# The last 64 keys of two successive pairs of heads in four 64x64 quadrants of TensorE

## The chip, the cores and the metric

The kernel runs on one core of one Trainium2 chip. The metric is the device time of one run in microseconds, the median of three runs.

## The reference

Attention with a sigmoid in place of the softmax, for 8 batches of 12 heads, 448 positions and 64 values a head:

```python
scores = scale * np.matmul(q, k.transpose(0, 1, 3, 2)) - np.log(S)   # scale 1/8, S 448
attn = 1.0 / (1.0 + np.exp(-scores))
x = np.matmul(attn, v)                                               # (8, 12, 448, 64)
```

The heads are put side by side (x is 8 x 448 x 768 then). Behind it stands a mixing of positions through rank 32 and a feed forward of width 3072:

```python
h = x.transpose(0, 2, 1) @ U @ V            # U 448 x 32, V 32 x 448
u = x + h.transpose(0, 2, 1)
out = u + np.maximum(u @ w_ch1, 0.0) @ w_ch2   # 768 x 3072, 3072 x 768
```

The keys of a head are 448 = 3 x 128 + 64: three full blocks and the last 64.

## The kernel before, in words

**Layout.** Everything is held transposed: features on the 128 partitions, the 448 positions as columns. Two heads of 64 features fill the partitions, so a batch has six pairs of heads, and one tile of 128 x 448 for each. The sigmoids of one block of 128 keys stand with the keys on the partitions and two heads' 448 positions side by side as columns (128 x 896).

**Attention of one pair** (`pair`, with `scores_of` and `values_of`). The scores of a block of keys (L500) take, for each head, the 64 partitions of that head; the two heads' matmuls use the upper and the lower half of the array's rows. ACT makes the sigmoid of each head (L588). The values of the first three blocks (L514) use all 128 rows, and each head 64 of the columns, both into one bank. The last 64 keys are the fourth block, j = 3: its score matmul yields 64 rows for each head, its two sigmoids have 64 partitions each, head 0 in the upper and head 1 in the lower half of one 128 x 448 tile, and its value matmul (L519) is one full 128 x 128 matmul for both heads, with a v tile that the host has laid out with zeros in the other head's places. ACT copies the result bank into the pair's tile of u (`ua` or `ub`), and for batches 1 to 7 DVE takes its maximum.

Batches 0 and 1 do this in float32. Batches 2 to 7 split every operand into two float16 halves, high and low, after scaling, and do three products (high by high, low by high, high by low) in place of one. For this POOL writes the high half (`scaled`) and DVE the rest (`rest`, L367) of q, k and v into a staging buffer `stg` (two buffers, all of a pair's halves in one), after ACT has summed absolute values to find the scales (`bound`, L420, whose wide output is written to a tile `junk` that nothing reads). The sigmoids are split too: L609 copies the high half on ACT, L367 writes the rest on DVE.

**Mixing** (L660 to L762). Once a batch's pairs are in u, they are transposed (xnt holds the transposed halves), multiplied with U and V, and added to u; u is then split into halves `us` for the feed forward.

**Feed forward.** W1 and W2 come as int64 words that hold float64 values. In batch 0, `decode` loads each group's weights in pieces of 128 x 768 words (`w`<-`w_in`, L344, through a ring of three buffers `w64`), DVE packs them to float32 (`to_f32`, two operations a piece), ACT bounds them (L420), and DVE and ACT split them to halves; they are also stored to scratch memory and read back for the later batches. Batches 0 to 3 run the plain products: 18 matmuls a chain in L836 (W1), 12 a chain in L856 (W2), six groups of weights a batch, W1 of a group one step ahead of its W2. Batches 4 to 7 are done two at a time by a scheme of seven products on quarters (L1031) at the end of the program, where no attention is left.

**What sets the order.** The program is written as a list of operations, each with an engine, a cost in us that is a number of the table at the top or at the call, a position in time (`pos`), and the tiles it reads and writes. `Plan.order` places them: it repeatedly takes the engine that can start first, and on it, of the operations that could start by then, the one with the least position. A tile gets its buffer out of a ring when its first user is placed. The result is a fixed order of instructions for each engine, and a fixed order of DMA issues on SP; at run time each engine works its list off in this order and waits where something is late. TensorE's operations carry the shape of array they begin and end with (`modes`): a change of shape costs `SWITCH` in the plan, and while the array is in a smaller shape an operation that begins with the same one is preferred by `BOND`.

The attention of batch 0 is at the start of the program, that of batch 1 beside the feed forward of batch 0, and those of 2, 4, 3, 5, 6, 7 beside the feed forward of batches 1 to 3. Eight banks of results are shared: the feed forward has four while batch 0 runs and three later (`PF`), attention the other four, and later five (`PS_`). The sigmoid tiles have six buffers for the wide blocks and two for the narrow one (`A2`, `A1`), the float32 ones before the split two and one (`AT2`, `AT1`).

## Time and profile before

| | |
|---|---|
| runs | 1572.27, 1572.36, 1574.84 us |
| median | 1572.36 us |
| the profiled execution's own time | 1575.69 us |
| its span in the profile | 1573.9 us |
| TensorE busy | 1550.3 us (99%), 8711 matmuls |
| VectorE (DVE) | 1129.4 us (72%) |
| ScalarE (ACT) | 850.6 us (54%) |
| GpSimd (POOL) | 381.4 us (24%) |
| DMA | 319.37 MB, 203 GB/s on average |
| TensorE's granted clock | 0.997 |

The profile is one execution. The span runs from its first to its last instruction; the time of the run is 1.8 us more. Tile names in the rows are the program's. Their buffer number is left out where a group holds several. A row with a line number in its form "x18" stands for a run of 18 like instructions.

### The profile page before, as it was taken

Reading aid. Unit: us, or ns where it says so; the run is one execution under the profiler, and the core shown is the slowest. Engines: PE = TensorE matmul, PEld = TensorE weight load, DVE = VectorE, ACT = ScalarE, POOL = GpSimd, SP = SyncE. Lnnn points to the kernel's source line nnn. Section 1 sums busy time; section 2 is a strip of 40 time slices with the busy share of each in tenths; the row PEclk is TensorE's granted clock in tenths of the full one; section 3 lists DMA queues with packets and bytes.
Section 4 is the critical chain, followed back from the end, with each engine's and each line's share of the span. In section 5 each row is a group of like instructions: output and inputs, shape, how many; then the busy total and the mean of one; then the engine's idle time right before and its main releaser. Section 6 shows DMA issues by size and latency. Waiting matters only on the chain.

```text
span 1573.9 us, 23648 instructions
## 1 busy us (share of the span) xinstructions
PE 1550.3 (99%) x8711; PEld 764.0 (49%) x8711; DVE 1129.4 (72%) x1886; ACT 850.6 (54%) x1521; POOL 381.4 (24%) x465
## 2 busy tenths in 40 slices
PE   8999999999999999999999999999999899999999
PEld 3344455544444544444444445555555455555554
DVE  2899999766777768777677766687776668564656
ACT  7666755478687668687698763242332614121310
POOL 0100001741222552132122254246551500000000
PEclk9999999999999999999999999999999999999999
DMA  8698888988867788655677549977673573333321
GB/s 231 191 315 280 282 291 254 317 233 196 206 192 184 222 261 225 159 154 160 187 211 189 144 149 285 315 246 247 220 248 126 176 255 132 106 109 136 107 106 71
DMA packets 208724, 319.37 MB, mean 203 GB/s; under 512 B 126176, under 2 KB 174688, under 8 KB 196320
## 3 DMA queue, kind: packets, MB, share of 16 engines
q1 hardware_dynamic: 208608, 317.86, 65.2%
q8 instruction: 68, 1.11, 0.3%
q14 instruction: 48, 0.39, 0.1%
HBM read 246.25 MB, written 77.42 MB: 206 GB/s over the span
## 4 chain that ended last, share of the span: by engine, by line
PE 91%; DVE 3%; DMA 2%; issue 1%; POOL 1%; SPq 1%; ACT 1%; POOLq 0%; DVEq 0%; ACTq 0%
PE bank L1031 36%; PE bank L856 20%; PE bank L836 19%; PE bank L500 7%; PE bank L514 5%; PE bank L519 2%; DMA w<-w_in 2%; PE bank L753 1%; DMA v__102<-v_in 1%; SPq L344 1%; DVE stg__107 L367 1%; PE bank L762 0%; DVE us__87 L367 0%; DVE xnt L367 0%; DVE us__86 L367 0%
## 5 line engine op out<-in xcount | busy, mean ns | idle before, releaser
L367 DVE SCALAR_TENSOR_TENSOR a<-at,a 128x896 f16<-128x896 f32 (+1 forms) x144 | 142.0, 1004 | 38.6 <-ACT a L609 38.2
L856 PE MATMUL bank<-h__93,w__91 128*128 128x448 f16 x792 | 159.9, 355 | 0.0
L856 PE MATMUL bank<-h__92,w__90 128*128 128x448 f16 x792 | 158.8, 353 | 0.0
L836 PEld LDWEIGHTS <-w__89 128*128 128x128 f16 x936 | 90.5, 98 | 89.4 <-issue 7.6
L856 PEld LDWEIGHTS <-w__91 128*128 128x128 f16 x864 | 83.6, 98 | 82.8 <-issue 9.1
L856 PEld LDWEIGHTS <-w__90 128*128 128x128 f16 x864 | 83.1, 98 | 82.1 <-issue 7.7
L609 ACT ACTIVATE a<-at 128x896 f16<-128x896 f32 (+1 forms) x144 | 116.9, 858 | 0.4
L1031 PEld LDWEIGHTS <-w__88 128*128 128x128 f16 x819 | 80.1, 98 | 74.7
L836 PEld LDWEIGHTS <-w__88 128*128 128x128 f16 x792 | 76.8, 98 | 74.6 <-issue 4.6
L1031 PEld LDWEIGHTS <-w__91 128*128 128x128 f16 x756 | 74.0, 98 | 74.0 <-issue 5.2
L1031 PEld LDWEIGHTS <-w__89 128*128 128x128 f16 x756 | 74.0, 98 | 69.0
L919 POOL TENSOR_TENSOR w<-w 128x384 f32<-128x384 f32 x96 | 104.7, 1091 | 5.1
L836 PE MATMUL bank<-us__87,w__89 128*128 128x448 f16 x504 | 99.7, 353 | 0.0
L1031 PEld LDWEIGHTS <-w__90 128*128 128x128 f16 x693 | 67.8, 98 | 63.3
L836 PE MATMUL bank<-us__86,w__89 128*128 128x448 f16 x432 | 85.3, 353 | 1.7 <-DVE ua__75 L367 1.7
L836 PE MATMUL bank<-us__86,w__88 128*128 128x448 f16 x432 | 84.8, 353 | 0.0
L588 ACT ACTIVATE at<-bank,bias_s,c__221 128x448 f32<-128x448 f32 (+1 forms) x96 | 65.0, 723 | 16.4 <-PE bank L500 7.0
L915 POOL TENSOR_TENSOR w<-w 128x384 f32<-128x384 f16 x48 | 45.7, 981 | 112.9 <-DVE xnt L923 70.6
L836 PE MATMUL bank<-us__87,w__88 128*128 128x448 f16 x360 | 70.9, 353 | 0.0
L588 ACT ACTIVATE at<-bank,bias_s,c__223 128x448 f32<-128x448 f32 (+1 forms) x96 | 64.5, 724 | 10.7 <-PE bank L500 10.0
L588 ACT ACTIVATE at<-bank,bias_s,c__222 128x448 f32<-128x448 f32 (+1 forms) x96 | 65.1, 722 | 5.9 <-DVE a L367 2.6
L843 ACT ACTIVATE r__94<-bank 128x448 f32<-128x448 f32 x48 | 25.9, 539 | 64.9 <-PE bank L836 64.9
(1167 smaller groups left out, 3130.2 us busy)
## 6 DMA issues: line engine op xcount, KB each, us to landing
w<-w_in SPq DMA_DIRECT2D x48, 768.0 KB, 5.9
forms<-xnt SPq DMA_DIRECT2D x24, 768.0 KB, 4.8
w__88<-forms SPq DMA_DIRECT2D x13, 1344.0 KB, 6.3
w__89<-forms SPq DMA_DIRECT2D x12, 1344.0 KB, 5.8
w__91<-forms SPq DMA_DIRECT2D x12, 1344.0 KB, 5.8
w__89<-scratch SPq DMA_DIRECT2D x10, 1536.0 KB, 7.9
w__90<-forms SPq DMA_DIRECT2D x11, 1344.0 KB, 5.8
forms<-scratch SPq DMA_DIRECT2D x144, 96.0 KB, 4.1
```

What stands on the lines that cost most here:

```text
L367: nc.vector.scalar_tensor_tensor(out=out, in0=in0, scalar=s, in1=in1, op0=op0, op1=op1)
L500: nc.tensor.matmul(o, keys, y[rows_of(h)], start=i == 0, stop=i == n - 1)
L514: nc.tensor.matmul(av.x[rows_of(h), :S], x[:, j, rows_of(h)], y(tiles[j], h), start=j == 0 and i == 0, stop=False, skip_group_check=True,)
L519: nc.tensor.matmul(av.x[:, :S], x[:, 3, :], y(tiles[3], 0), start=False, stop=i == n - 1, skip_group_check=True)
L588: act(cost, lambda: nc.scalar.activation(out_(), in_(), AF.Sigmoid, bias=bias_s[rows], scale=c if whole else c.x[rows]), kin + ["bias"] + ...
L609: act(0.57 if j == 3 else 0.95, lambda a=a, to=to: nc.scalar.activation(half(a, 0), to.x, AF.Copy, scale=A_UP), kto, [(a, 0)], here + A_OFF)
L836: nc.tensor.matmul(ph.x[:, :S], wx[:, x, c, f * P : (f + 1) * P], us.x[:, c, y, :], start=c == 0 and i == 0, stop=c == NP - 1 and i == 2,)
L843: act(0.54, lambda: nc.scalar.activation(r.x, ph.x[:, :S], AF.Relu, scale=DOWN_H), [ph], [r], pos - EV_IN)
L856: nc.tensor.matmul(po.x[:, :S], wx[:, x, f, e * P : (e + 1) * P], h.x[:, f, y, :], start=f == 0 and i == 0, stop=f == FC - 1 and i == 2,)
L915: pool(1.0, lambda j=j: nc.gpsimd.tensor_tensor(out=t.x[:, j], in0=quarter(j, 0), in1=quarter(j, 1), op=ALU.add), [(w, j, 0), (w, j, 1)] i ...
L919: pool(1.0, lambda o_=o_, x=x, y=y, sub=sub: nc.gpsimd.tensor_tensor(out=t.x[:, o_], in0=t.x[:, x], in1=t.x[:, y], op=ALU.subtract if sub ...
L1031: nc.tensor.matmul(bank.x[:, :S], wt.x[:, k, FACTOR[n], x], both(f)[:, y], start=start and k == i == 0, stop=k == 2 and i == 2, skip_group ...
```

## The change

The last 64 keys are now done once for two successive pairs of one batch, an even one and the odd one behind it: four heads. The even pair does its three full blocks alone. With the odd pair, four 64x64 matmuls a product make the scores of the last 64 keys: the head gives the 64 rows of the array and the pair the 64 rows of the result (pair m's keys go to rows 64m of bank h). So one sigmoid of 128 partitions for each head number serves both pairs, on two full tiles of 128 x 448; its scale differs for the two halves, and POOL assembles it in a new 128 x 1 tile `cm`, half by half. The value matmuls of the last 64 keys are four 64x64 matmuls a product, two into the even pair's bank and two into the odd pair's. The even pair's bank therefore stays taken until then, and both pairs' copies to u follow the odd pair's values. L519 and its zero-padded full matmul are gone; the new lines are L526 (scores) and L551 (values).

What goes with it:

- Rings. The staging buffer becomes three rings in one tile: `STQ` (q and k, three), `STV` (v's first 384 keys, two), `V3` (the last 64 keys of two pairs, two). The sigmoids have seven wide tiles, and no narrow ones.
- Loads. q and k of a pair are one DMA of 128 x 448 each in place of two of 64 x 448. A new small DMA writes the last 64 keys of both heads, without the zeros, over the half of the v tile that is used (`ends`); it is issued after the v load and writes into the same tile.
- Banks. Feed forward has three and attention five from the start.
- `bound` writes the absolute values of the weights into the piece's own `w64` buffer, whose words have been packed by then, and not into `junk`.
- `mix_half` runs after pairs 3 and 5 of a batch, since only odd pairs complete u; before it ran after 2 and 5.
- Score operations also follow the score operation before them in the plan, scale tiles have a depth of three (one for `uv`) by name.
- The table of numbers at the top differs, and with it most positions.

```diff
-ROOM0, ROOM, AHEAD, BEFORE, PACE = 36.845, 55.576, 45.387, 23.39, 0.896
+ROOM0, ROOM, AHEAD, BEFORE, PACE = 43.832, 36.166, 43.931, 23.228, 0.522
...
-START, DECODE = 59.42, 44.285
+START, DECODE = 46.389, 44.263
...
+    A2 = [Buffer(a_[:, 2 * i * S : 2 * (i + 1) * S]) for i in range(7)]
...
+    for n in (STQ_N,) * 3 + (STV_N,) * 2 + (V3_N,) * 2:
...
-    PF, PS_ = [BANK[:4]] + [BANK[:3]] * (B - 1), [BANK[4:]] * 2 + [BANK[3:]] * (B - 2)
+    PF, PS_ = [BANK[:3]] * B, [BANK[3:]] * B
...
+    def bound(x, n, o, kx, ko, pos, cost, to=None):
+
+        act(cost, lambda: nc.scalar.activation((to.x.bitcast(BF16) if to else junk)[:, :n], x(), AF.Abs, accum_out=o()), kx, [ko] + ([to] if to else []), pos)
...
+        def ends():
+            x = v[b, p]
+            return bass.AP(tensor=x.tensor, offset=x.offset + 3 * P, ap=[[4 * P, D], [4 * P * D + D, 2], [1, D]])
+
+        load(lambda: v32.x[mine, 3].rearrange("k (h d) -> k h d", h=2), ends, D * P * 4, [], [(v32, 1)], early + 0.2)
...
+                for i in range(n):
                     for h in range(2):
+                        if j < 3:
+                            x, y = products[-1]()[i]
+                            nc.tensor.matmul(sc[j, h].x[:, :S], x[rows_of(h), j * P : j * P + P], y[rows_of(h)], start=i == 0, stop=i == n - 1)
+                            continue
+                        for m in range(2):
+                            x, y = products[m]()[i]
+                            nc.tensor.matmul(sc[j, h].x[rows_of(m), :S], x[rows_of(h), 3 * P : S], y[rows_of(h)], start=i == 0, stop=i == n - 1)
...
-            for i, (x, y) in enumerate(products()):
-                nc.tensor.matmul(av.x[:, :S], x[:, 3, :], y(tiles[3], 0), start=False, stop=i == n - 1, skip_group_check=True)
...
+            for i in range(n):
+                for m in range(2):
+                    x, y = quad["last"][m]()[i]
+                    for h in range(2):
+                        nc.tensor.matmul(avs[m].x[rows_of(h), :S], x[rows_of(m), rows_of(h)], y(tiles[3], h)[rows_of(m)],
+                                         start=False, stop=i == n - 1, skip_group_check=True)
...
-        for n, j in enumerate((3, 0, 1, 2)):
-            here = at + (d * (n // 2) / SECOND if b else 0.0)
+        for j in range(3 + odd):
+            here = at + (d * (j // 2) / SECOND if b else 0.0)
...
-                sc = scores_of(b, ((3, 0), (1, 2))[n // 2], score_products, kscore, here, b == 0 or b == 1 and p < 2)
+                sc = scores_of(b, (j, j + 1) if j == 0 or odd else (j,), products, kj, here, early)
...
-            bound(lambda t=t: t.x, PIECE, lambda n=n: ss.x[:, n : n + 1], [t], (ss, n), pos + n, 1.03)
+            bound(lambda t=t: t.x, PIECE, lambda n=n: ss.x[:, n : n + 1], [t], (ss, n), pos + n, 1.03, w64)
...
-            if b >= WHOLE and p % 3 == 2:
-                mix_half(b, p // 3, start + (MIXED - 5 + p) * d)
+            if b >= WHOLE and p in (3, 5):
+                mix_half(b, p // 5, start + (MIXED - 5 + p) * d)
```

How the order moves, at three places. First TensorE near the start, the attention of batch 0 in float32. Line numbers here and below are of each kernel's own file: L500 and L522 are scores, L526 the new quadrant scores, L514 and L541 the values of the first 384 keys, L519 and L551 those of the last 64. Before, the values of two pairs and the scores of a third:

```order
L514 MATMUL bank4_113<-a_96,v1__102 64x448 x6
L519 MATMUL bank4_113<-a_96,v1__102 128x448
L514 MATMUL bank5_114<-a_96,v2__103 64x448 x6
L519 MATMUL bank5_114<-a_96,v2__103 128x448
L500 MATMUL bank1_110<-qk0__98 64x448
L500 MATMUL bank2_111<-qk0__98 64x448
L500 MATMUL bank3_112<-qk0__98 128x448
```

Changed, an even pair's first values, the quadrant scores of both pairs, and later the odd pair's values with the last 64 keys of both:

```order
L541 MATMUL bank4_112<-a_96,v0__101 64x448 x6
L526 MATMUL bank5_113<-qk0__98 64x448
L526 MATMUL bank5_113<-qk1__99 64x448
L526 MATMUL bank6_114<-qk0__98 64x448
L526 MATMUL bank6_114<-qk1__99 64x448
L522 MATMUL bank7_115<-qk2__100 128x448
...
L541 MATMUL bank6_114<-a_96,v1__102 64x448 x6
L551 MATMUL bank4_112<-a_96,v0__101 64x448 x2
L551 MATMUL bank6_114<-a_96,v1__102 64x448 x2
```

Each pair had its own block of 64 keys, right behind its values; now one block stands for two pairs, and bank 4 of the even pair is held until the odd pair's values are through.

Second, SP's queue of loads while batch 0's weights stream in. Before, with the semaphores each load waits for:

```order
L344 DMA qk__99<-k_in 64x448 [waits DMAHW3_49,PE_49]
L344 DMA qk__99<-q_in 64x448 [waits DMAHW4_49]
L344 DMA scratch_0_143<-w__90 128x6144 [waits DMAHW5_49,DVE_49,Activation_49]
L344 DMA w_106<-w_in 128x768 [waits DMAHW6_49,DVE_49]
L344 DMA qk__100<-k_in 64x448 [waits DMAHW7_49,PE_49]
L344 DMA w_106<-w_in 128x768 [waits DMAHW0_49,DVE_49]
```

And changed:

```order
L359 DMA v__103<-v_in 128x512 [waits DMAHW2_49,PE_49]
L359 DMA v__104<-v_in 128x512 [waits DMAHW3_49,PE_49]
L963 DMA forms_0_127<-scratch_0_136 128x3x128 [waits DMAHW4_49]
L963 DMA forms_0_127<-scratch_0_136 128x3x128 [waits DMAHW5_49]
L359 DMA v__103<-v_in 64x2x64 [waits DMAHW6_49,DMAHW2_49]
L359 DMA scratch_0_142<-w__90 128x6144 [waits DMAHW7_49,DVE_49]
L359 DMA v__104<-v_in 64x2x64 [waits DMAHW3_49,DMAHW0_49]
L359 DMA w_106<-w_in 128x768 [waits DMAHW1_49,Activation_49]
L359 DMA w_106<-w_in 128x768 [waits Activation_49] x2
```

The weights' loads wait for ACT in place of DVE, and the small v loads of 64x2x64 wait for the v load of their own tile (the second semaphore of the two). In front of a load stands the order of SP, in which nothing overtakes.

Third, DVE near the end of batch 0's weights. `w01__89` is the tile of W1's last group, `xnt` and `ub` belong to the mixing of batch 1. Before, the last split of W1 (four pieces, with its scale `s_w1`) and what follows it:

```order
L367 SCALAR_TENSOR_TENSOR w01__89<-at_97,s_w1__192,w01__89 128x768 x2
L367 SCALAR_TENSOR_TENSOR w01__89<-us1__87,s_w1__192,w01__89 128x768 x2
L367 SCALAR_TENSOR_TENSOR xnt_105<-bank4_113,s_x0__203,xnt_105 128x384
L367 SCALAR_TENSOR_TENSOR xnt_105<-bank7_116,s_x0__203,xnt_105 64x384
...
L367 SCALAR_TENSOR_TENSOR ub0__80<-bank7_116,kap0__206,ub0__80 128x448
```

Changed, the mixing's last steps, the split of an earlier group, and then the last split:

```order
L382 SCALAR_TENSOR_TENSOR ub3__83<-bank7_115,kap0__199,ub3__83 128x448
L382 SCALAR_TENSOR_TENSOR ub4__84<-bank6_114,kap0__199,ub4__84 128x448
L440 TENSOR_REDUCE mx1__155<-ub3__83 128x1
L440 TENSOR_REDUCE mx1__155<-ub4__84 128x1
L382 SCALAR_TENSOR_TENSOR ub5__85<-bank5_113,kap0__199,ub5__85 128x448
...
L382 SCALAR_TENSOR_TENSOR w01__89<-us1__87,s_w0__184,w01__89 128x768 x3
L382 SCALAR_TENSOR_TENSOR w01__89<-stg_107,s_w0__184,w01__89 128x768
...
L382 SCALAR_TENSOR_TENSOR w01__89<-at_97,s_w1__185,w01__89 128x768 x2
L382 SCALAR_TENSOR_TENSOR w01__89<-stg_107,s_w1__185,w01__89 128x768 x2
```

The mixing of batch 1 (transposed halves, additions, maxima) stood behind W1's last split and stands ahead of it now.

184 lines of the change are left out of this document (109 added, 75 removed).

## The prediction

> **What bounds the kernel now.** I read the page first: busy time and the chain that ended last.
>
> ```profile
> span 1573.9 us, 23648 instructions
> PE 1550.3 (99%) x8711; PEld 764.0 (49%) x8711; DVE 1129.4 (72%) x1886; ACT 850.6 (54%) x1521; POOL 381.4 (24%) x465
> ...
> PE 91%; DVE 3%; DMA 2%; issue 1%; POOL 1%; SPq 1%; ACT 1%; POOLq 0%; DVEq 0%; ACTq 0%
> ```
>
> TensorE is busy for 1550.3 of 1573.9 us and makes 91% of the chain, so the first question of any edit is how much TensorE time it removes and where. The busy time by stage (window, its length, then PE, PEld, DVE, ACT and POOL busy, TensorE's clock, DMA share) says where that time is really the limit.
>
> ```profile
> 0.00:60.00 60.00, 54.21 (x227) 20.39 (x228) 26.30 (x45) 40.72 (x78) 2.26 (x9) 1.00 0.84 244
> ...
> 86.00:262.00 176.00, 170.07 (x875) 83.58 (x874) 166.71 (x296) 113.23 (x217) 4.50 (x7) 0.99 0.83 286
> ...
> 306.00:990.00 684.00, 682.02 (x4250) 331.66 (x4249) 487.34 (x819) 493.50 (x882) 219.22 (x298) 1.00 0.71 201
> ```
>
> From 306 to 990 us, where the attention of batches 2 to 7 lies, TensorE is at 682.0 of 684 us and DVE and ACT at 487 and 494. There a matmul less is time less. From 86 to 262 us it is different: TensorE 170.1 of 176 and DVE 166.7 of 176. That is the stage in which DVE turns the int64 weights into halves, and the feed forward of batch 0 eats them as they come. What TensorE saves there is worth something only if DVE also ends sooner.
>
> For the prices I read TensorE's instructions in order of time (start, length, line, shape, count).
>
> ```profile
> 401.08 1.89 PE L514 MATMUL bank<-a,stg__108 128*64 128x448 f16 x18
> 402.90 0.74 PE L519 MATMUL bank<-a,stg__108 128*128 128x448 f16 x3
> 403.48 2.43 PE L856 MATMUL bank<-h__92,w__90 128*128 128x448 f16 x12
> ...
> 407.25 3.57 PE L836 MATMUL bank<-us__87,w__89 128*128 128x448 f16 x18
> 410.75 1.31 PE L500 MATMUL bank<-stg__107 64*128 64x448 f16 x12
> 411.99 2.44 PE L856 MATMUL bank<-h__92,w__90 128*128 128x448 f16 x12
> ...
> 433.44 3.57 PE L836 MATMUL bank<-us__87,w__88 128*128 128x448 f16 x18
> 436.85 0.27 PE L382 MATMUL bank<-ident,mm_u__166 128*128 128x128 f32 x1
> ```
>
> Eighteen full matmuls run from 433.44 to 436.85 when the next one needs no other shape of array: 0.1894 us each. The same 18 take 3.50 before a 64-row piece (407.25 to 410.75): 0.09 more for the change. The 12 score matmuls (64*128, two side by side) take 1.24, which is six times 0.1894 and 0.10; the 18 value matmuls (128*64, two side by side) take 1.82, nine times 0.1894 and 0.12. So a unit of work is 0.1894 us, pairs of halves overlap completely, in rows as in columns, and a change of shape costs 0.10.
>
> **The change, part by part.** The half-precision attention first (batches 2 to 7: 36 pairs of heads, so 18 couples, as I call two successive pairs).
>
> ```profile
> L500 PE MATMUL bank<-stg__107 64*128 64x448 f16 x432 | 47.1, 351 | 0.0
> ...
> L514 PE MATMUL bank<-a,stg__107 128*64 128x448 f16 x324 | 34.1, 355 | 0.0
> ...
> L519 PE MATMUL bank<-a,stg__107 128*128 128x448 f16 x54 | 13.3, 356 | 0.0
> ```
>
> The second staging buffer has a row of the same count for each, so there are 864 score, 648 column-half value and 108 full value matmuls now. Scores: 864/2 = 432 units become 648/2 + 216/4 = 378. Values: 648/2 + 108 = 432 become 648/2 + 216/4 = 378. That is 108 units less, **20.5 us**, if four quadrants run side by side as two halves do. The trace has no four at once. The cheapest it can be is one unit for four; the dearest is two at a time, one unit for two, and then nothing at all is gained (108 units come back). I take the cheap end, because rows of both kinds, two halves by rows and two by columns, show full overlap, and four quadrants read and write no more partitions in a unit than either of them.
>
> The new pieces need more changes of shape: in the whole order of TensorE I count 266 now and 283 after, 17 more, **+1.7 us**. Bounds: 0, if adjoining pieces hide them, and 24 couples with two each, 4.8.
>
> Float32 attention (batches 0 and 1, six couples):
>
> ```profile
> 80.53 2.48 PE L514 MATMUL bank<-a,v__104 128*64 128x448 f32 x12
> 82.94 1.02 PE L519 MATMUL bank<-a,v__104 128*128 128x448 f32 x2
> ```
>
> Twelve records, two for each matmul and so three units of 128 keys, run from 80.53 to 82.94; less 0.10 for the change of shape that is 0.77 a unit. Each couple loses one unit of the scores and one of the values, 12 in all, **9.2 us**. Batches 0 and 1 are worked off before 262 us, where the weights decide. I charge this gain at 0: what covers it is DVE's decoding, and if that cover goes (DVE early) the 9.2 come on top.
>
> The table of numbers also moves work, and in the early stage this matters. DVE waits for the weights' DMA hardly at all there (engine, waited for, us, times, longest):
>
> ```profile
> DVE stg__108 L364 <- DMA w<-w_in: 1.5, 2, 1.0
> ```
>
> Now the last split of W1's group 5, the matmuls that use it, and the end of feed forward 0 (the last from the chain of waits):
>
> ```profile
> 248.93 1.95 DVE L367 SCALAR_TENSOR_TENSOR w__89<-us__87,s_w__192,w__89 128x768 f16<-128x768 f32 x2
> ```
> ```profile
> 259.59 3.57 PE L836 MATMUL bank<-us__86,w__89 128*128 128x448 f16 x18 [1.69 <-DVE ua__75 L367]
> ```
> ```profile
> 303.88 2.38 PE bank L856 x12
> 306.25 3.41 PE bank L836 x18
> ```
>
> The split ends at 248.93 + 1.95 = 250.9, TensorE starts on it at 259.6 after a wait, and the last chain of batch 0 ends at 306.25. In the changed order the mixing of batch 1 stands ahead of this split on DVE, where now most of it is behind. The rows that change sides (count, mean ns):
>
> ```profile
> L367 DVE SCALAR_TENSOR_TENSOR xnt<-bank,s_x__203,xnt 128x384 f16<-128x384 f32 x6 | 3.6, 612 | 0.0
> ...
> L367 DVE SCALAR_TENSOR_TENSOR xnt<-bank,s_x__203,xnt 64x384 f16<-64x384 f32 x2 | 1.2, 599 | 0.0
> L367 DVE SCALAR_TENSOR_TENSOR xnt<-bank,xnt 32x384 f16<-32x384 f32 x2 | 1.1, 550 | 0.1
> ...
> L367 DVE SCALAR_TENSOR_TENSOR ub__81<-bank,kap__206,ub__81 128x448 f32<-128x448 f32 x1 | 0.7, 683 | 0.7 <-PE bank L701 0.7
> ...
> L367 DVE SCALAR_TENSOR_TENSOR us__87<-ub__80,s_u__174,us__87 128x448 f16<-128x448 f32 x1 | 0.7, 674 | 0.0
> ```
>
> Eight xnt splits (4 of 0.612, 2 of 0.599, 2 of 0.550: 4.7), six adds of 0.68 (4.1), six maxima, which I estimate at 0.6 like these (3.7), and six us splits of 0.674 and more (at least 4.0): 16.5 us. The split of group 5 then ends near 267. Behind it TensorE's order has 216 matmuls until batch 0 is done (group 5 in, the next batch's group 0 in, group 5 out), 40.9 us: 308, against 306.25. **+1.9 us**, and the 9.2 of float32 have become waiting in front of that split. Bounds: -9.2 if DVE runs 11 us ahead of this (it is busy 26.3 of the first 60 us, so there is room), +12 by the ring, below.
>
> Two waits are new on SP's queue. The weights' buffer is now also the place where ACT's absolute values go, so the next load waits for ACT and not for DVE; and a second, small v load writes into the first one's tile, so it waits until that has landed, and SP's loads behind it wait too.
>
> ```profile
> 97.18 3.78 SPq L344 DMA_DIRECT2D w<-w_in  x2
> ```
> ```profile
> 100.70 0.84 ACT L420 ACTIVATE junk<-stg__108 128x768 bf16<-128x768 f32 x1 [1.65 <-DVE stg__108 L367]
> 101.45 0.19 ACT L420 ACTIVATION_READ_ACCUMULATOR junk<-stg__108 128x1 f32 x1
> ```
> ```profile
> w<-w_in SPq DMA_DIRECT2D x37, 768.0 KB, 5.9
> ...
> v__104<-v_in SPq DMA_DIRECT2D x2, 256.0 KB, 7.1
> ```
>
> The second of these two loads leaves SP by 100.96, when DVE has released the buffer; ACT's two rows on the same piece end at 101.64. I take 1.0 us of longer hold a piece. Three buffers, 37 loads in this stage: 1.0/3 x 37 = 12 us if the ring is the limit, 0 if the loads stay ahead, as the 1.5 us of waits above say. What the v loads add on SP is of the same kind: one lands 7.1 us after its issue, and the rows behind it stand for what is left of that. I take 0, the nearer end by the waits, and keep +12 for the range.
>
> The rest I put at nothing. Fourteen sigmoids a couple in place of sixteen, and two q and k loads a pair in place of four: less work on ACT, and on SP as much as the new v load adds. POOL gets two small operations more a pair (at 219 of 684 us busy it has room), DVE one of 64 partitions for each pair and one wide split in place of two narrow ones. The even pair's output bank stays taken until the odd pair is done: then the odd pair's last four score banks wait for all four sigmoids of the first set, where one bank was spare. A chain of feed forward (2.4 to 3.5 us in the rows above) stands between the two sets and hides it; without it, one sigmoid a couple shows:
>
> ```profile
> L588 ACT ACTIVATE at<-bank,bias_s,c__222 128x448 f32<-128x448 f32 (+1 forms) x96 | 65.1, 722 | 5.9 <-DVE a L367 2.6
> ```
>
> 0.72 x 18 = 13 us.
>
> The sum, on the profiled execution (1575.7 us in the list of times, 1573.9 of span): 1575.7 - 20.5 + 1.7 + 0 + 1.9 = 1558.8. That execution stands 3.3 us over the median of 1572.36, so **1555.5**, 1556 rounded.
>
> **Rivals.** *The early stage pays as well.* DVE is ahead by 11 us or more: then TensorE's own work is the limit from the start, the 9.2 of float32 count and the 1.9 do not: 1572.4 - 20.5 + 1.7 - 9.2 = 1544. For it: 33.7 idle us of DVE in the first 60, and the faster float32 pairs free q and k buffers sooner. Against it: that idleness comes from loads, which gain little.
>
> *The ring of weights is the limit.* 12 us later: 1568; half of it, 1562. For it: loads leave SP at the moment DVE frees a buffer. Against it: 1.5 us of DVE waiting in 176.
>
> *Quadrants go two at a time*, on the slower side: nothing saved, 1.7 + 1.9 added: 1576. It decides from the first couple on, in every couple. The Trainium skill (TensorE: Matmul & The Clock Gate, section "Part 3: Packing small matmuls — row/col tiling") says a weight load overlaps running matmuls only when its row group differs; two of four quadrants share theirs, and by that rule this rival is what happens. The trace speaks against it:
>
> ```profile
> L836 PEld LDWEIGHTS <-w__89 128*128 128x128 f16 x936 | 90.5, 98 | 89.4 <-issue 7.6
> ...
> L514 PEld LDWEIGHTS <-stg__108 128*64 128x64 f16 x324 | 16.8, 109 | 16.0 <-issue 5.9 <-POOL inv_qkv__216 L364 0.4
> ```
>
> The value matmuls of 128 rows share all row groups, their loads take 109 ns (a full one 98), and 18 of them still take nine units. The same page's section "LDWEIGHTS (loading the stationary operand)" prices a load at its columns over 1.2, 53 ns for 64; four in a row would be 213 ns a unit and not 189, and the sum 1558 (an estimate from that page).
>
> *The late v loads stall the main stage.* TensorE does less and the 36 waits on SP put v later. The stage has one such stall now:
>
> ```profile
> 748.25 9.41 DMA v__102<-v_in
> ```
> ```profile
> 760.22 0.74 PE L762 MATMUL bank<-vst,xnt 128*128 128x448 f16 x3 [1.98 <-DVE xnt L367]
> 760.80 4.12 PE L856 MATMUL bank<-h__93,w__91 128*128 128x448 f16 x12
> ```
>
> The v load took 9.41 us to land, the mixing behind it came late, TensorE waited 1.98 us and its next 12 matmuls took 4.12 instead of 2.43: 3.7 us. Four more make 15 us: 1571.
>
> **Chances.** First reading (1556, own range 1550 to 1562): 0.46. Early stage pays: 0.25. Ring: 0.15. Late v: 0.08. Two at a time: 0.06. A gain under 0.2% (3.1 us, about what a measurement here can tell from no change) comes only with half of late v, 0.02 of the ring and 0.01 of two at a time: same 0.07. The other 0.05 of two at a time is slower: 0.05. The rest is faster: 0.46 + 0.25 + 0.13 + 0.04 = 0.88. The range leaves out the ends of the ring and late-v cases and a little of the early one: 1542 to 1569.
>
> **What would show it.** Quadrant pieces: 12 matmuls in 0.57 us between starts, plus 0.10 for the change; at 1.14 the rival of two holds. A couple's TensorE time falls by 1.1 less its changes. Busy TensorE over the run near 1522. Batch 0's last chain near 308; at 297 the early stage has paid, at 320 the ring or the v loads hold DVE, and DVE's waits for the weights' DMA in 86 to 262 us would be near 12 in place of 1.5. I am wrong if TensorE shows idle gaps of several us after 310 us behind ACT or v loads, or if the half-precision couples do not shrink.

## The result: 1872.94 us, and the profile after

| | before | changed |
|---|---|---|
| median | 1573.15 us (1572.27 to 1574.84, 4 runs) | 1872.94 us (1869.03 to 1875.27, 4 runs) |
| ratio | | 1.1902, 95% interval 1.1877 to 1.1926 |
| TensorE busy | 1550.3 us of 1573.9 | 1607.3 us of 1867.2 |

The kernel became 300 us slower; 1556 was forecast. The page of the changed kernel, its span, busy times and the chain that ended last:

```profile
span 1867.2 us, 23943 instructions
PE 1607.3 (86%) x8843; PEld 772.0 (41%) x8843; DVE 1120.4 (60%) x1904; ACT 813.2 (44%) x1455; POOL 383.9 (21%) x537
...
PE 53%; DMA 23%; DVE 8%; ACT 4%; issue 3%; SPq 1%; POOL 1%; ACTq 0%; POOLq 0%; DVEq 0%
```

DMA was 2% of the chain before and is 23% now, and TensorE's share fell from 91% to 53%. By stage (window, length, then PE, PEld, DVE, ACT and POOL busy, TensorE's clock, DMA share, GB/s), first before, then changed:

```profile
0.00:306.00 306.00, 292.51 (x1423) 134.91 (x1424) 253.75 (x455) 189.31 (x355) 43.60 (x54) 0.99 0.81 268
306.00:990.00 684.00, 682.02 (x4250) 331.66 (x4249) 487.34 (x819) 493.50 (x882) 219.22 (x298) 1.00 0.71 201
990.00:1580.00 590.00, 575.75 (x3042) 297.42 (x3040) 388.31 (x612) 167.81 (x285) 118.58 (x114) 1.00 0.50 169
```
```profile
0.00:306.00 306.00, 203.83 (x921) 85.68 (x922) 163.94 (x299) 131.41 (x258) 11.55 (x22) 0.84 0.55 183
306.00:990.00 684.00, 570.18 (x3318) 266.46 (x3317) 388.07 (x679) 347.62 (x626) 173.19 (x287) 0.90 0.55 166
990.00:1868.00 878.00, 833.31 (x4607) 419.85 (x4605) 568.35 (x928) 334.18 (x573) 199.18 (x228) 0.97 0.53 173
```

TensorE idles 102 us of the first 306 (13.5 before), 114 of the next 684 (2.0 before) and 44 of the rest (8.1 before). DMA's share is lower than before in the first two windows, and yet DMA is waited for. How both can be shows in the first 24 us. The rows are the DMA's busy share in tenths and its rate, in 40 slices of 0.6 us. Before:

```profile
GB/s 0 0 0 72 167 191 179 207 273 304 167 221 204 217 348 304 317 347 293 284 263 227 279 229 288 343 351 302 198 272 237 276 210 321 381 282 268 201 221 158
```

Changed:

```profile
DMA  0000011118911111111111111489599941111111
GB/s 0 0 0 15 9 30 45 51 51 122 358 51 48 51 51 48 51 51 48 51 52 47 51 51 48 109 338 205 114 332 346 343 128 48 48 51 51 48 54 55
```

For slice after slice the changed kernel moves 47 to 52 GB/s. Over the stretch from 6.6 to 15.0 us the mean is 50 GB/s at a DMA share of 0.13, and two of 16 engines are 0.125. TensorE waits (start, length, and in brackets the idle time before it and what ended it):

```profile
12.95 4.75 PE L522 MATMUL bank<-qk__98 64*128 64x448 f32 x12 [12.95 <-DMA qk__98<-q_in]
23.60 4.54 PE L522 MATMUL bank<-qk__99 64*128 64x448 f32 x12 [5.90 <-DMA qk__99<-q_in]
```

Before, its first matmul started at 4.31 us. Later the loads of q and k hold ACT, which sums their absolute values first (engine, waited for, us, times, longest):

```profile
ACT junk L436 <- DMA qk__100<-q_in: 81.6, 12, 12.6
ACT junk L436 <- DMA qk__99<-q_in: 56.4, 12, 6.5
ACT junk L436 <- DMA qk__98<-k_in: 43.3, 8, 6.9
```

The loss has a second part. The span grew by 304.9 us over that of a kernel told of below whose only difference is the shape of these loads (flat, 1562.3 us); TensorE's idle time grew by 219.9 and its busy time by 85.0, with the same matmuls. One group, the scores in halves, in the changed kernel and in that other one:

```profile
L522 PE MATMUL bank<-stg 64*128 64x448 f16 x648 | 91.0, 387 | 66.0 <-ACT at L638 38.5 <-ACT ub__80 L678 16.4 <-ACT ub__82 L678 5.2
```
```profile
L518 PE MATMUL bank<-stg 64*128 64x448 f16 x648 | 74.5, 351 | 1.7 <-ACT ub__81 L674 1.6
```

The same 648 matmuls take 387 ns each in place of 351. The granted clock is 0.84 and 0.90 in the first two windows above, where TensorE waits, against 0.96 and 1.00 in flat, whose windows follow below. At the end of the program, where no attention is left, the matmuls of the feed forward take 352 ns in the changed kernel and 352 or 353 in flat.

### The profile page after: what moved, and what is told of

It reads as the page before. It is cut to its first block, busy times and chain, and to the rows that moved or that the text cites. A ratio compares the mean times of both kernels' runs of the same rounds, so it can differ in the third digit from the quotient of the medians.

```text
span 1867.2 us, 23943 instructions
## 1 busy us (share of the span) xinstructions
PE 1607.3 (86%) x8843; PEld 772.0 (41%) x8843; DVE 1120.4 (60%) x1904; ACT 813.2 (44%) x1455; POOL 383.9 (21%) x537
## 4 chain that ended last, share of the span: by engine, by line
PE 53%; DMA 23%; DVE 8%; ACT 4%; issue 3%; SPq 1%; POOL 1%; ACTq 0%; POOLq 0%; DVEq 0%
PE bank L1096 31%; PE bank L921 9%; PE bank L901 8%; DMA qk__99<-q_in 6%; DMA qk__100<-q_in 3%; DMA qk__98<-k_in 2%; DMA qk__98<-q_in 2%; PE bank L522 2%; DMA v__101<-v_in 2%; DVE stg L382 2%; DMA v__102<-v_in 2%; PE bank L541 1%; DMA w<-w_in 1%; ACT at L638 1%; DVE a L382 1%
## 5 line engine op out<-in xcount | busy, mean ns | idle before, releaser
L382 DVE SCALAR_TENSOR_TENSOR a<-at,a 128x896 f16<-128x896 f32 x126 | 137.8, 1113 | 80.3 <-ACT a L668 79.7
L921 PE MATMUL bank<-h__92,w__90 128*128 128x448 f16 x792 | 176.5, 380 | 8.6 <-DVE h__92 L910 3.9
L921 PE MATMUL bank<-h__93,w__91 128*128 128x448 f16 x792 | 163.0, 361 | 10.1 <-ACT h__92 L909 7.6
L522 PE MATMUL bank<-stg 64*128 64x448 f16 x648 | 91.0, 387 | 66.0 <-ACT at L638 38.5
L901 PEld LDWEIGHTS <-w__89 128*128 128x128 f16 x864 | 85.9, 101 | 123.5 <-issue 43.4
L921 PEld LDWEIGHTS <-w__90 128*128 128x128 f16 x864 | 87.4, 104 | 108.8 <-issue 45.0
L921 PEld LDWEIGHTS <-w__91 128*128 128x128 f16 x864 | 84.5, 100 | 96.5 <-issue 24.8
L901 PEld LDWEIGHTS <-w__88 128*128 128x128 f16 x864 | 84.8, 99 | 91.2 <-issue 17.5
L668 ACT ACTIVATE a<-at 128x896 f16<-128x896 f32 x126 | 116.3, 960 | 0.6
L901 PE MATMUL bank<-us__86,w__89 128*128 128x448 f16 x432 | 92.5, 372 | 24.1 <-DVE mm_w__176 L837 12.2
L1096 PEld LDWEIGHTS <-w__89 128*128 128x128 f16 x819 | 80.1, 98 | 74.8
L1096 PEld LDWEIGHTS <-w__88 128*128 128x128 f16 x756 | 74.0, 98 | 69.0
L1096 PEld LDWEIGHTS <-w__91 128*128 128x128 f16 x756 | 74.0, 98 | 69.0
L984 POOL TENSOR_TENSOR w<-w 128x384 f32<-128x384 f32 x96 | 100.5, 1047 | 4.9
L901 PE MATMUL bank<-us__87,w__89 128*128 128x448 f16 x432 | 89.5, 364 | 7.2 <-ACT h__93 L909 7.2
L1096 PEld LDWEIGHTS <-w__90 128*128 128x128 f16 x693 | 67.8, 98 | 63.3
L901 PE MATMUL bank<-us__86,w__88 128*128 128x448 f16 x432 | 87.8, 361 | 7.0 <-ACT h__92 L909 7.0
L901 PE MATMUL bank<-us__87,w__88 128*128 128x448 f16 x432 | 85.8, 355 | 0.0
L541 PE MATMUL bank<-a,stg 128*64 128x448 f16 x648 | 76.1, 385 | 1.9 <-ACT at L638 1.6
L522 PEld LDWEIGHTS <-stg 64*128 64x128 f16 x648 | 29.0, 98 | 117.7 <-issue 101.2
L638 ACT ACTIVATE a<-bank,bias_s 128x448 f32<-128x448 f32 x84 | 47.5, 634 | 39.3 <-PE bank L522 37.3
```

The lines of the kernel that those rows point to most:

```text
L382: nc.vector.scalar_tensor_tensor(out=out, in0=in0, scalar=s, in1=in1, op0=op0, op1=op1)
L522: nc.tensor.matmul(sc[j, h].x[:, :S], x[rows_of(h), j * P : j * P + P], y[rows_of(h)], start=i == 0, stop=i == n - 1)
L541: nc.tensor.matmul(av.x[rows_of(h), :S], x[:, j, rows_of(h)], y(tiles[j], h), start=j == 0 and i == 0, stop=not quad and j == 2 and i == n ...
L638: act(cost, lambda: nc.scalar.activation(out_(), in_(), AF.Sigmoid, bias=bias_s, scale=c if whole else by.x), kin + ["bias"] + ([] if whol ...
L668: act(0.95, lambda a=a, to=to: nc.scalar.activation(half(a, 0), to.x, AF.Copy, scale=A_UP), kto, [(a, 0)], here + A_OFF)
L901: nc.tensor.matmul(ph.x[:, :S], wx[:, x, c, f * P : (f + 1) * P], us.x[:, c, y, :], start=c == 0 and i == 0, stop=c == NP - 1 and i == 2,)
```

## The experiments

Idle time below is a window's length less TensorE's busy time in it.

**The shape of the q and k loads.** Theory S: the load's source has two rows in its outer dimension, so only two DMA engines share it. Rival W: SP's queue is blocked by the second v load and by the weights' buffers. Every ratio is to the kernel before in the same set of runs on the same chip. There were three sets, on two chips; before's median was 1573.19, 1573.94 and 1572.36 us in them, so a difference of medians from two sets is uncertain by 1 or 2 us. The first kernel is the changed kernel with plain 128-row loads, called flat below:

```diff
...
-                return bass.AP(tensor=x.tensor, offset=x.offset, ap=[[2 * S * D + S, 2], [2 * S, D], [1, S]])
...
-            load(lambda i=i: qk.x[:, i], heads_of, P * S * 4, [], [(qk, i)], early)
+            load(lambda i=i: qk.x[:, i], lambda src=src: src[b, p], P * S * 4, [], [(qk, i)], early)
...
-        x = np.asarray(x).reshape(B, NP, 2, S, D).transpose(0, 1, 4, 2, 3)
-        return np.ascontiguousarray(np.concatenate([x, x], axis=2))
+        x = np.asarray(x).reshape(B, NP, 2, S, D).transpose(0, 1, 2, 4, 3)
+        return np.ascontiguousarray(x.reshape(B, NP, P, S))
```

> The changed kernel with one thing different: the host lays q and k out so that a pair's tile is one plain block of 128 rows of 448, and the load of q or k reads it as 128 rows; before it was a source of two outer rows of 64 rows each. Same bytes, same number of loads, same order on every engine. Theory S (the two outer rows put the whole load on few of the 16 DMA engines, and every load behind it in their queues is late): nearly all of the 300 us goes, 1556 as first forecast, 1545 to 1575. The Trainium skill (DMA: Bandwidth & Descriptors, section on why a DMA increments its semaphore by 16 and not by 1) says that the number of engines is the largest up to 16 that divides the slowest dimension of both sides, here 2. Rival W (SP's order is blocked by the second v load, which waits for the first, and by weights' buffers that ACT holds longer): the loads of q and k are not the cause, and the time stays above 1800.

Measured: 1566.72 us (1564.04 to 1568.72), ratio to before 0.996 (0.9944 to 0.9976). The order on TensorE and DVE is the changed kernel's. It is 306 us less than that one, so without this shape of load the change is 6.5 us faster than before. Its windows:

```profile
0.00:306.00 306.00, 275.14 (x1400) 127.10 (x1401) 244.91 (x445) 177.00 (x338) 32.46 (x49) 0.96 0.81 272
306.00:990.00 684.00, 678.58 (x4440) 328.37 (x4439) 498.39 (x853) 468.62 (x837) 235.95 (x375) 1.00 0.68 208
990.00:1580.00 590.00, 568.60 (x3007) 293.80 (x3004) 381.53 (x607) 166.93 (x280) 119.09 (x114) 1.00 0.48 162
```

Then the reverse, only this load put into the kernel before (before_merged):

```diff
-        for h in range(2):
-            for i, src in ((1, k), (0, q)):
-                load(lambda i=i, h=h: qk.x[rows_of(h), i, :], lambda src=src, h=h: src[b, p, rows_of(h), h, :],
...
+                return bass.AP(tensor=x.tensor, offset=x.offset, ap=[[2 * S * D + S, 2], [2 * S, D], [1, S]])
+
+            load(lambda i=i: qk.x[:, i], heads_of, P * S * 4, [], [(qk, i, 0), (qk, i, 1)], early)
```

> The kernel before with one thing different: two loads a pair with the source of two outer rows (as the change has them) in place of four of 64 rows. Nothing else of the change is in it. Theory S: slower by most of what the change lost, 1750 to 1900. Rival W: 1568 to 1578, since neither the second v load nor the longer hold of the weights' buffers is in it.

Measured: 1881.66 us (1880.52 to 1882.72), ratio 1.1963 (1.1945 to 1.1981). It has no quadrant, no second v load and no longer hold of weights, and loses 308 us. The rate in its first 24 us:

```profile
GB/s 0 0 0 9 18 39 42 45 67 177 289 51 51 51 48 51 51 48 54 48 53 46 51 48 71 280 329 283 353 309 182 65 51 48 51 51 48 52 61 41
```

The same floor: 50 GB/s on average from 7 to 13 us, at a share of 0.13. W falls: the load alone makes the loss and its removal alone undoes it.

What in the load does it? Two kernels keep a source of three levels with gaps, but with 16 and with 4 outer rows (G), in the order of flat (outer16, outer4):

```diff
+        return bass.AP(tensor=x.tensor, offset=x.offset, ap=[[(P // G + 1) * S, G], [S, P // G], [1, S]])
...
+        x = x.reshape(B, NP, G, P // G, S)
+        return np.ascontiguousarray(np.concatenate([x, x[:, :, :, :1]], axis=3))
```

> The kernel with plain 128-row loads of q and k, but the source has 16 outer rows of 8 rows with a gap behind each eight, so that it stays a source of three levels as in the change. Same order. Theory S (what counts is the number of outer rows, since it is the number of DMA engines that share the load): 1563 to 1571, no difference to 1566.7. Rival G (a source of three levels, or one with gaps, is slow by itself): near 1873.

Measured: 1571.08 us (1567.13 to 1574.91), ratio 0.9992 (0.9979 to 1.0004), 0.1 us above the range that theory S gave and 302 us below rival G.

> The same with four outer rows of 32. Theory S: four engines share a load, so about 100 GB/s while such a load is alone in flight against the 48 to 51 GB/s of the changed kernel's start, and a time between 1566.7 and 1873, nearer to the first (some of the 2.3 us that a load of 224 KB then takes is hidden): 1580 to 1700. Rival G: as with 16, whatever that is.

Measured: 1672.9 us (1670.08 to 1674.64), ratio 1.0636 (1.062 to 1.0652). Its first 24 us:

```profile
DMA  0001224784986222224969995221231257999986
GB/s 0 0 0 24 54 69 76 148 290 143 165 181 251 88 101 102 102 96 146 232 211 291 306 244 173 114 102 61 55 30 48 78 143 286 326 215 275 291 190 130
```

Where such a load is alone, from 8.4 to 10.8 us, the mean rate is 100 GB/s and the share 0.26 (4 of 16 is 0.25). So 2 outer rows give 50 GB/s and 1873 us, 4 give 100 and 1673, 16 give 1571, and 128 give 1567: some 25 GB/s for each outer row of the first two. Rival G falls, as 16 rows with the same gaps lose nothing of that size. (The 4 us between 16 and 128 stay open: the two kernels ran in different sets, and the intervals of their ratios to before, 0.9979 to 1.0004 and 0.9944 to 0.9976, nearly meet.) The Trainium skill (DMA: Bandwidth & Descriptors, "Why a DMA increments its semaphore by 16 and not by 1") says that the engines of a load are the largest number up to 16 that divides the slowest dimension of both sides. By that rule 2, 4 and 16 outer rows use 2, 4 and 16 engines; the shares of 0.13 and 0.26 agree for the first two, and for 16 only the time speaks, as no load of that kind is alone in its trace.

**The number of loads.** The change also has two loads of 128 rows in place of four of 64. Four in the changed kernel, first with four operations in the plan (four):

```diff
+            for h in range(2):
+                load(lambda i=i, h=h: qk.x[rows_of(h), i, :], lambda src=src, h=h: src[b, p, rows_of(h), h, :],
+                     D * S * 4, [], [(qk, i, h)], early)
```

and then with the order kept, two operations of two loads each (four_same):

```diff
+            def two(i=i, src=src):
+                for h in range(2):
+                    nc.sync.dma_start(out=qk.x[rows_of(h), i, :], in_=src[b, p, rows_of(h), h, :])
+
+            op("SP", max(0.6, P * S * 4 / 0.30e6), two, [], [(qk, i)], early, land=2.0)
```

> The changed kernel with the loads of q and k as they were in the kernel before: four of 64 rows a pair in place of two of 128. The order on SP differs a little by the two added loads. Theory S: 1550 to 1580, near the kernel of plain 128-row loads; if the number of loads on SP counts, some us above it. Rival W: above 1800.

> The changed kernel with four q and k loads of 64 rows a pair, as before, but the plan is told of two loads of 128: so the order on every engine is the change's, with two loads in place of each. The kernel of the first set that had four loads in the plan too took 1625.5, with plain 128-row loads 1566.7. If the 59 us between them come from two more issues a pair on SP: near 1620. If they come from the other order that the plan makes of the same table when it counts four loads: 1564 to 1575.

Measured: four 1625.48 us (1622.75 to 1627.11), ratio 1.0332 (1.0316 to 1.0349); four_same 1580.42 us (1576.66 to 1582.28), ratio 1.0037 (1.0024 to 1.0051). Of the 58.8 us between four and flat, 13.7 come from the loads themselves in an unchanged order, and 45.1 from the other order that the plan makes when it counts them (12 and 46 by the ratios, as four_same is of another set). The expectation had the two as alternatives, near 1620 or 1564 to 1575; both take part, the order with three quarters. Where in that order the 45 us go stays open. With four half loads the quadrants' gain is more than eaten.

The same in the kernel before, with flat's host layout: two plain loads a pair, once in the plan (before_flat) and once with before's order kept (before_same, where the first of each two operations loads all 128 rows and the second nothing).

```diff
+                def whole(i=i, src=src, h=h):
+                    if h == 0:
+                        nc.sync.dma_start(out=qk.x[:, i, :], in_=src[b, p])
```

> The kernel before with two plain loads of 128 rows a pair in place of four of 64 (host layout as in the first kernel of this set). It prices the smaller number of loads on SP alone. SP is not what TensorE waits for in the profile before, so 1568 to 1576, no change that can be told; if issues on SP held the first 60 us back, 1560 to 1567.

> The kernel before with one full load of 128 rows in place of every two half loads of q or k, and the order on every engine kept: the plan is still told of four loads. The kernel of the first set in which the plan knew of it took 1585.6. Four half loads in place of two cost the changed kernel's order 13.7 us (1580.4 against 1566.7), so if the number of loads on SP counts there too: 1560 to 1568, and only the rest of the gain is the quadrants'. If before's order hides them: 1571 to 1576.

Measured: before_flat 1585.59 us (1584.11 to 1589.42), ratio 1.0085 (1.0064 to 1.0106); before_same 1570.41 us (1568.83 to 1572.39), ratio 0.9989 (0.998 to 0.9997). In before's own order fewer loads are worth some 2 us: the time is 0.6 us under the range of the second reading, in which that order hides them. The order that the plan makes without them costs 15. Before_flat was expected unchanged: I had not thought of the plan's order, which shifts with every operation that is added or taken away. So from here on edits kept the order wherever they could.

**The second v load, and the hold of the weights' buffers.** Both in flat with its order kept. For the first, the host puts the last 64 keys where they are needed and the operation issues nothing (noends):

```diff
-        load(lambda: v32.x[mine, 3].rearrange("k (h d) -> k h d", h=2), ends, D * P * 4, [], [(v32, 1)], early + 0.2)
+        op("SP", max(0.6, D * P * 4 / 0.30e6), lambda: None, [], [(v32, 1)], early + 0.2, land=2.0)
...
-        vl[:, :, h * 64 : h * 64 + 64, 3, cols] = v5[:, :, h, 384:]
+        for m in range(2):
+            vl[:, m::2, m * 64 : m * 64 + 64, 3, cols] = v5[:, m::2, h, 384:]
```

> The kernel with plain 128-row loads of q and k, and one thing different: the host puts the last 64 keys of v where the odd or the even pair needs them, so the second small v load into the same tile is gone, and with it its wait for the first. The order of all else is the same. If these waits hold SP's queue back: 3 to 8 us less than 1566.7, most of it after 310 us if the late v loads stall the main stage. If they lie behind other work, as the trace of that kernel shows at one wait of 1.9 us between 60 and 310 us: within 2 of 1566.7.

Measured: 1557.66 us (1555.15 to 1558.85), ratio 0.9897 (0.9883 to 0.991); 9.1 us less than flat (10 by the ratios). In flat's chain of waits stood (start, length):

```profile
505.41 8.22 DMA v__101<-v_in
513.64 5.33 DMA v__101<-v_in
...
519.78 0.53 ACT ub__84 L674
520.36 0.54 PE bank L823 x2
```

The v load of 8.2 us is followed by the small one into the same tile, 5.3 us more. ACT, which works in a fixed order, sums the absolute values of this v before it copies `ub__84`, and the mixing on TensorE (L823) follows that copy. From 306 us on ACT's waits for v loads add up to 23.3 us in flat and 0.5 in noends. What TensorE waits for from 306 us on, in flat (the two largest) and in noends (all):

```profile
PE bank L823 <- DVE xnt L382: 2.8, 1, 2.8
PE bank L518 <- ACT ub__81 L674: 1.6, 1, 1.6
```
```profile
PE bank L537 <- ACT at L634: 0.3, 1, 0.3
```

And the windows of noends:

```profile
0.00:306.00 306.00, 275.99 (x1404) 127.38 (x1405) 245.65 (x446) 177.15 (x338) 33.48 (x51) 0.96 0.80 270
306.00:990.00 684.00, 683.62 (x4471) 331.51 (x4470) 502.73 (x864) 471.63 (x841) 236.43 (x373) 1.00 0.70 208
990.00:1580.00 590.00, 561.95 (x2972) 290.55 (x2969) 376.06 (x596) 164.86 (x277) 118.63 (x114) 1.00 0.47 160
```

Idle time behind 306 us falls from 9.1 to 4.0 us, in front of it from 30.9 to 30.0. The first reading of this expectation holds, somewhat beyond its 8 us. (The two profiled executions are 6.7 us of span apart, as flat's is the fastest of its runs.)

The hold of the buffers, with the absolute values really written to the separate tile, which is made larger for it (hold):

```diff
-        act(cost, lambda: nc.scalar.activation((to.x.bitcast(BF16) if to else junk)[:, :n], x(), AF.Abs, accum_out=o()), kx, [ko] + ([to] if to else []), pos)
+        act(cost, lambda: nc.scalar.activation(junk[:, :n], x(), AF.Abs, accum_out=o()), kx, [ko] + ([to] if to else []), pos)
```

> The kernel with plain 128-row loads of q and k (first set), and one thing different: ACT's absolute values of the weights are really written to the separate tile and not into the weights' own buffer, so a load of weights waits for DVE's packing and not for ACT. The order on every engine is that of the first set's kernel, since the plan is still told of the old place. Theory H (the ring of weights is what makes the end of batch 0 late, 312.9 us there against 306.3 before): batch 0 ends near 306 and the time falls by 5 to 8, to 1560. Theory M (the order on DVE makes it late: the mixing of batch 1 ahead of the last split of W1): within 2 of 1566.7, batch 0 near 312.

Measured: 1567.43 us (1563.98 to 1569.3), ratio 0.9959 (0.9947 to 0.9972): no difference to flat's 1566.72. SP's waits from 60 to 310 us, in flat and in hold:

```profile
SPq L359 <- ACT w L436: 82.9, 35, 6.5
```
```profile
SPq L359 <- ACT junk L436: 2.0, 2, 1.5
```

The waits for ACT fell from 82.9 to 2.0 us, but most of them became waits for DVE: all of SP's waits for DVE in this stretch add up to 56.5 us in flat and 127.4 in hold. So ACT held the buffers only a little longer than DVE did. The end of batch 0 moved from 312.9 to 311.5 us, not to 306, and the time stayed. Theory H falls.

**The mixing ahead of the last split.** One number of the table in flat (PACE 1.2 for 0.522; pace):

> The kernel with plain 128-row loads of q and k, and one number of the table different (PACE 1.2 for 0.522), which spreads the attention of batch 1 over more of batch 0 and puts its mixing behind the last split of W1 on DVE, as it mostly was before. The order changes elsewhere too. Theory M: batch 0 ends 4 to 9 us sooner, near 306, and where the rest stays as it is the time is 1557 to 1563. Theory H: batch 0 still near 312. If the table only fits its own order, the time can rise behind batch 0, which the end of batch 0 in the trace then tells apart.

Measured: 1565.18 us (1561.0 to 1566.62), ratio 0.994 (0.9926 to 0.9954). In flat the last split of W1 ends at 271.5 us and batch 0's last chain at 312.9; in pace the latter ends at 287.8 (DVE and TensorE in order of time: flat, flat, pace):

```profile
269.52 1.94 DVE L382 SCALAR_TENSOR_TENSOR w__89<-stg,s_w__185,w__89 128x768 f16<-128x768 f32 x2
```
```profile
288.90 10.38 PE L897 MATMUL bank<-us__87,w__88 128*128 128x448 f16 x54
299.12 13.78 PE L917 MATMUL bank<-h__93,w__91 128*128 128x448 f16 x72
```
```profile
278.56 9.24 PE L917 MATMUL bank<-h__93,w__91 128*128 128x448 f16 x48
287.64 3.57 PE L897 MATMUL bank<-us__87,w__88 128*128 128x448 f16 x18
```

Twenty-five us sooner, and 1.5 us in the whole, within the spread. So neither theory's time came: M gave 1557 to 1563. The end of batch 0 was the wrong thing to look at. Batch 1's first four chains of W1 (`us__87`, `w__88`, 72 matmuls, 13.6 us at 0.1894 each) stand ahead of it in flat and behind it in pace, so this part of the work has only changed places. Idle time is what counts. Before 306 us it falls from 30.9 in flat to 22.4, and behind it rises from 9.1 to 12.9.

```profile
0.00:306.00 306.00, 283.60 (x1467) 132.13 (x1468) 256.26 (x460) 185.12 (x353) 41.43 (x60) 0.99 0.82 278
306.00:990.00 684.00, 676.21 (x4399) 325.65 (x4397) 498.75 (x843) 462.65 (x827) 233.56 (x363) 1.00 0.68 206
990.00:1580.00 590.00, 564.05 (x2981) 291.44 (x2979) 385.62 (x603) 164.71 (x277) 120.16 (x114) 1.00 0.47 161
```

With the second v load gone too (the diffs of noends and pace together), the last kernel (best):

> The changed kernel with plain 128-row loads, without the second v load, and with PACE 1.2 in place of 0.522: the two edits of the second set together. In that set, without the second v load TensorE idled 30 us before 306 us and 4 behind; with PACE 1.2 alone 22 and 13. If the 13 came from the late v loads, both gains add: 1546 to 1553. If the slower pace itself makes the later idling: 1553 to 1560.

Measured: 1551.66 us (1550.27 to 1555.02), ratio to before 0.987 (0.9854 to 0.9886), as expected where both gains add. It is faster than before, as the whole interval is below 1. Its windows:

```profile
0.00:306.00 306.00, 284.69 (x1458) 131.72 (x1459) 255.08 (x458) 183.08 (x350) 41.37 (x60) 0.97 0.80 275
306.00:990.00 684.00, 682.09 (x4453) 330.19 (x4452) 504.35 (x859) 467.56 (x835) 228.92 (x363) 1.00 0.68 208
990.00:1580.00 590.00, 555.70 (x2936) 287.04 (x2934) 379.69 (x589) 161.88 (x272) 120.12 (x114) 1.00 0.46 158
```

Idle before 306 us is 21.3 and behind it 7.0. So 5.9 of pace's 12.9 late us came from the late v loads. Of the rest noends, with the faster pace, has 4.0 too, and 3.0 go with the slower pace.

## Why the prediction was wrong, and where it was right

The same accounting for each kernel (median; then, of the profiled execution, span, TensorE busy, its idle time before and behind 306 us):

| kernel | median | span | busy | idle to 306 | idle behind |
|---|---|---|---|---|---|
| before | 1573.15 | 1573.9 | 1550.3 | 13.5 | 10.1 |
| changed | 1872.94 | 1867.2 | 1607.3 | 102.2 | 157.7 |
| flat | 1566.72 | 1562.3 | 1522.3 | 30.9 | 9.1 |
| noends | 1557.66 | 1555.6 | 1521.6 | 30.0 | 4.0 |
| best | 1551.66 | 1550.8 | 1522.5 | 21.3 | 7.0 |

**The step that failed** is in the paragraph "The rest I put at nothing", where "two q and k loads a pair in place of four" were costed as less work. They were counted as issues on SP; the shape of the transfer was put at nothing without a reason. It is 306 us (1872.94 against 1566.72). The changed kernel's source has the two outer rows (the lines shown ahead of the prediction leave this load out), and the profile before has no load of that kind, so its cost had to be bounded like that of every operation which the trace doesn't show. At the 50 GB/s that the changed kernel then showed, a load of 224 KB takes 4.6 us, and there are 96 of them: 440 us with nothing hidden. An estimate beforehand, by the rule of the Trainium skill quoted above (DMA: Bandwidth & Descriptors, same section; two of 16 engines) and the mean of 203 GB/s before, would have been 9 us a load and over 800 in all. No rival of mine looked there. "Late v loads stall the main stage" named the wrong load and 15 us. The prediction's own sign of being wrong, gaps on TensorE behind 310 us, did come: 158 us of idle time behind 306.

**Quadrants** hold. Scores and values of the last 64 keys in noends, each with the start of what follows:

```profile
396.98 0.76 PE L522 MATMUL bank<-stg 64*64 64x448 f16 x12
397.67 3.58 PE L897 MATMUL bank<-us__87,w__89 128*128 128x448 f16 x18
...
416.38 0.76 PE L547 MATMUL bank<-a,stg 64*64 64x448 f16 x12
417.08 3.58 PE L897 MATMUL bank<-us__87,w__89 128*128 128x448 f16 x18
```

Twelve quadrant matmuls take 0.69 and 0.70 us from start to start: three units of 0.19 and the change of shape. The rival of two at a time (1.14 and the change) falls. Between the second four and the third four of such a row the trace has 0.189 us in the mean of all 36 rows, so the loads of 64 columns side by side do not cost the 213 ns a unit of the other estimate.

**TensorE's busy time** holds in the sum: 20.5 less in half precision, 9.2 less in float32 and 1.7 more for changes of shape make 28.0, and 1550.3 - 1522.3 (flat) is 28.0. The exactness is luck. Beside the 74.5 of the scores shown above, flat's half-precision attention has these groups:

```profile
L537 PE MATMUL bank<-a,stg 128*64 128x448 f16 x648 | 68.2, 355 | 0.3 <-ACT at L634 0.3
L522 PE MATMUL bank<-stg 64*64 64x448 f16 x216 | 13.7, 357 | 0.0
L547 PE MATMUL bank<-a,stg 64*64 64x448 f16 x216 | 13.7, 357 | 0.0
```

That makes 170.1 us against 189.0 before (two staging buffers of 47.1, 34.1 and 13.3): 18.9 less, as the 18.8 of the forecast. But the float32 attention, added up by its lines, fell from 92.3 to 77.2 us, 15.1 and not 9.2, and the remaining work took 6 us more, at a granted clock of 0.96 in place of 0.99 in the first 306 us.

**Float32's 9.2 us as waiting, and the mixing's 1.9**: the forecast was 11.1 us more idle in the early stage. Measured: 17.4 in flat and 16.5 in noends (30.9 and 30.0 against 13.5); so the early stage did not pay. In flat the split ended at 271.5 where I had it near 267, and the 216 matmuls behind it followed as counted (271.5 + 40.9 is 312.4; 312.9 measured). The direction was right and the size 5.4 us too small, by noends. That the order was to blame is not shown: pace takes 8.5 us of flat's idle time away but moves much else, too.

**The ring of weights**, taken at 0 with 12 as its bound: 0 in the time, 1.4 us at the end of batch 0 (hold). The longer hold mostly replaced waits for DVE. **The second v load**, taken at 0: 9.1 us (noends). The waits for the weights' DMA that I went by were DVE's in the early stage; the cost lay in the main stage, where ACT waits for v and the mixing stands behind it. **The even pair's bank**, at nothing behind a chain of feed forward: noends waits for 0.3 us in all behind 306 us, so it is hidden.

With the two loads mended the kernel takes 1557.66, against the 1555.5 of the sum. So the quadrants' part of the sum was right, for a kernel that the change wasn't; that the total is within 2 us is partly luck. TensorE's idle time is 5.4 us longer in the early stage than forecast and 6.1 us shorter behind it than before (4.0 against 10.1), which no term foresaw, and the two cancel.

## What to carry to other kernels

Price a transfer by its shape, not only by its bytes and its issue: look at the outermost dimension of both sides, and merge two loads into one only where the merged one still has many outer rows (16 were enough here, 4 cost 106 us). Where DMA is waited for while its mean share is low, look at rate and share over time: a floor (50 GB/s here) at a constant small share (0.13) points to few engines at work. In a planned kernel keep the order fixed when one cost is to be measured, since two load operations a pair more or less moved the whole by 45 and 15 us here; and judge a stage by TensorE's idle time, since the end of a stage moves with the work that is put into it.

## What the hardware showed that I had not expected

A load of 224 KB with two outer rows moved 50 GB/s, with four 100. The loads behind them did not fill the idle engines: in the changed kernel's first 24 us the share stays at one tenth for 14 slices in a row (0.6 us each, the first from 6.6 us on) and the v load that SP began to issue at 10.00 us took 4.48 us to issue, as the row below says; the rate rises only in the slice from 15 us on (SP's queue in order of time, start and length):

```profile
10.00 4.48 SPq L359 DMA_DIRECT2D v__102<-v_in  x1
```

Whether it waited for SP's issue or for its place in the engines' queues these runs don't tell apart. And where TensorE waited, it was also slower: with 102 of the first 306 us idle its granted clock was 0.84 on average, with 31 idle (flat) 0.96, and the same matmuls took 85 us more over the run, more than a quarter of the loss.
